# Ranking the first head pair's preparation and maxima ahead, its keys loaded by ScalarE's queue and its queries transposed first

## The chip, the cores and the metric

The kernel runs on one core of one Trainium2 chip. The metric is the device time of one execution in microseconds (us), lower is better; a set of runs is given by its median. An engine works through its own instructions strictly in the order in which the program lists them, and waits at an instruction whose inputs or buffers are not there yet.

## What is computed

Attention over pooled queries, followed by a feed-forward layer with softplus:

```python
q_pool = q.reshape(B, H, S // 2, 2, D).mean(axis=3)      # B=4, H=8, S=1152, D=64
scores = (1 / sqrt(D)) * q_pool @ k.T
scores = scores - scores.max(axis=-1)
attn = exp(scores); attn = attn / (attn.sum(axis=-1) + 1e-9)
x = (attn @ v), heads side by side                       # 2304 x 512
h = x @ w_in                                             # 512 x 2048
g = max(h, 0) + log1p(exp(-abs(h)))
out = g @ w_out                                          # 2048 x 512
```

All inputs and the output are float32 in the reference; the weights reach the kernel as 64-bit words and are decoded on the chip.

## The kernel before, in words

The work is cut into 16 units, u0 to u15, each one pair of heads of one batch, and into 8 blocks of rows of the feed-forward layer (U is the product with w_in and the softplus, D the product with w_out). For every unit there are three stages:

- **Preparation** (`prepare`, lines 540 to 649). The keys of the pair come by one DMA (L559) and the queries by six (L582 and L586) into two of the four `raw` buffers. Neighbouring queries are added (L348, the helper `tt_ways`). ScalarE takes the sum of squares of both (L437, the helper `squares`), a matmul with ones (L284) and four short VectorE instructions (L272, L292) make a power-of-two scale from them. Then keys and queries are each split into a high and a low float16 part: high by `hi_ways` (L315 on ScalarE, L319 on GpSimd, L272 on VectorE), low by `lo_ways` (L275 on VectorE). The two halves of the keys go into `kcat`, of which there is one, and a DMA transposes it into `kT` (L612); a further DMA copies its high part to `kB` (L618). The queries' high part goes into `qcat`, also one, and is transposed into `qA` (L625); their low part stays in `qlow`.
- **Maxima** (`maxima`, lines 652 to 736). The row maxima of the scores are found ahead of the attention. Per unit, 12 pairs of matmuls (L667) and 3 mixed pairs (L678) write 384 columns each into one of three PSUM banks `m`, and VectorE reduces each bank to one column (L688): 12 reduces for the first half of the rows, 15 for the second. When the 12 of the first half are there, L693 joins them, L272 and L275 (called at L696 and L698) put the result beside `qlow`, TensorE turns `qlow` (L713) and a copy (L733 on VectorE, or L730 on ScalarE) puts it into `qB`.
- **Attention** (`attention`, lines 762 to 890). For each half of the rows and each of nine key tiles: scores (L777 with `kT`, `qA`; L780 with `kB`, `qB`), the exponential on ScalarE (L787), the product with v (L795) and, in the first six units, the sums by TensorE (L802).

The order of the instructions is not written out by hand. Everything is a `task` with a rank (`prio`, the smaller goes first), the engines that could run it with a planned duration, and the tasks that it depends on. `Sched.run` plays this through once while the program is built: whenever an engine is free in that play, it takes the task of the smallest rank among those that are ready and whose buffers are free, and the instruction is then emitted. An engine is never kept free for a task that becomes ready a little later. DMAs are played as one server, `nbytes / 300 + 180` ns each, in their order of rank. So a changed rank can change the order of every later instruction, on every engine.

Ranks count key tiles of the attention: u0 starts at 0, u1 at 18, u2 at 36. A unit's preparation is ranked from the start of the unit before it (`x.was`, -18 for u0, 0 for u1, 18 for u2): loads at `was - 20`, preparation at `was - 14`, the queries' high part and their transposition one later, the maxima from `was` on. The decoding of w_in is ranked at 8, 16, ... 64 (`w_in`, lines 448 to 478, with `decode`, lines 406 to 431), that of w_out from 54 on. For u0 this gives loads at -38, preparation at -32, queries at -31, maxima at -18 to -4.8 (the mixed ones -3.6 to -2.4), the joining of the halves at -10.8 and -3.6. For u1: loads at -20, preparation at -14, queries at -13, maxima from 0 on.

Of the kernel before, what the change touches and what calls it, by code (L numbers as in the profile page):

```python
# [42 lines left out]
class Sched:  # L43
# [17 lines left out]
    def task(self, ways, deps=(), prio=0.0, take=(), give=()):  # L61
        t = Task(ways, prio, list(take), list(give))
        for d in deps:
            if d is not None:
                d.after.append(t)
                t.deps += 1
        self.tasks.append(t)
        return t
# [87 lines left out]
def pe(n, cols):  # L156
    return n * (cols / 2.4 + 2.5)
# [27 lines left out]
def tile_attention_softplus_ffn(  # L185
# [166 lines left out]
    def load(fn, nbytes, deps, prio, take):  # L352
        return task([("DMA", dma(nbytes), fn)], deps, prio, take=take)
# [186 lines left out]
    def prepare(u):  # L540
# [13 lines left out]
        x.sc = c[8]  # L554


        prio = x.was - 14.0
        r, cat = Hold(raw_r), Hold(kcat_r)
        kl = load(lambda: nc.sync.dma_start(  # L559
            out=r.item[:, 0:1152].rearrange("p (h t d) -> p h t d", h=2, t=KT),  # L560
            in_=k[b, 2 * p:2 * p + 2].rearrange("h (p t) d -> p h t d", t=KT)),
            2 * S * D * 4, [], prio - 6.0, [r])
        qr, qc = Hold(raw_r, 2), Hold(qcat_r)

        def raw():
# [52 lines left out]
                nc.sync.dma_start(out=x.kB.item[0:D, ks], in_=x.kT.item[h * D:(h + 1) * D, ks])  # L618

        x.kB_done = task([("DMA", 1500.0, high_keys)], [x.k_done], prio + 4.0, take=[x.kB])  # L620
        prio += 1.0
        y = task(hi_ways(1152, lambda: (qc.item, twice(qs()), c[5]), ("ACT", "DVE"), 1.0), [both], prio)
        x.ql_done = task(lo_ways(576, lambda: (x.qlow.item[:, :, 0:D], qs(), c[5], qc.item[:, :, 0])),
                         [y], prio, take=[x.qlow], give=[qr])
# [27 lines left out]
    def maxima(x):  # L652
        half_done, begun = [], None
        for half in range(2):
            parts = []
            first, last = ((0, 4), (4, T))[half]
            for o, t in enumerate(range(2 * half, 2 * half + 2 + half)):
                for g in range(3):
                    prio = x.was + x.early * (7.2 * half + 3.6 * o + 1.2 * g * (t < 4) + 0.6 * g * (t == 4))
                    if t < 4:  # L660
                        ps = [Hold(m_r), Hold(m_r)]

                        def mm(t=t, g=g, ps=ps):
                            for h in range(2):
                                k0 = h * KT + 3 * g
                                hs = slice(h * D, (h + 1) * D)
                                nc.tensor.matmul(  # L667
                                    out=ps[h].item[:, 0:384], lhsT=x.qA.item[hs, PLACE[h, t]],
                                    rhs=x.kT.item[hs, k0:k0 + 3].rearrange("p a b -> p (a b)"),
                                    start=True, stop=True, tile_position=(h * D, 0))  # L670
                    else:
                        ps = [Hold(m_r)]

                        def mm(t=t, g=g, ps=ps):
                            for h in range(2):
                                k0 = h * KT + 3 * g
                                hs = slice(h * D, (h + 1) * D)
                                nc.tensor.matmul(  # L678
                                    out=ps[0].item[hs, 0:384], lhsT=x.qA.item[hs, MIX, hs],
                                    rhs=x.kT.item[hs, k0:k0 + 3].rearrange("p a b -> p (a b)"),  # L680
                                    start=True, stop=True, tile_position=(h * D, h * D))

                    y = task([("PE", pe(1, 384) + 130.0, mm)], [x.q_done, x.k_done, begun], prio,
                             take=ps if begun else ps + [x.nm3], give=[x.qA, x.kT])
                    begun = begun or y
                    for h, bank in enumerate(ps):
                        c = PLACE[h, t] if t < 4 else MIX
                        parts.append(task([("DVE", dve(384), lambda c=c, g=g, bank=bank: nc.vector.tensor_reduce(  # L688
                            out=x.nm3.item[:, c, g:g + 1], in_=bank.item[:, 0:384], axis=AX.X, op=ALU.max,
                            negate=True))], [y], prio, give=[bank]))  # L690
            prio = x.was + x.early * 7.2 * (half + 1)
            ts_ = slice(first, last)
            y = small(lambda ts_=ts_: nc.vector.tensor_reduce(  # L693
                out=x.nm.item[:, ts_], in_=x.nm3.item[:, ts_], axis=AX.X, op=ALU.min), parts, prio,
# [6 lines left out]
            half_done.append(y)  # L701
        x.qB_done = [[], []]
        for half, h in ((0, None), (1, 0), (1, 1)):
            prio = x.was + x.early * 7.2 * (half + 1) + 0.2
            ps = Hold(m_r)
            n = 320 if half else 512

# [54 lines left out]
    def attention(x):  # L762
        b, p = x.b, x.p
        gate = since("u", x.u)
        for i, (t0, t1) in enumerate(HALF):
            n = (t1 - t0) * 64
            pv, acc = Hold(pv_r), Hold(acc_r)
            before = None
            sums = None
            for kt in range(KT):  # L770
                prio = x.at + x.slow * (9.0 * i + kt)
                s, pt = Hold(s_r), Hold(p_r, 2)
# [1 line left out]
                def scores(kt=kt, s=s, t0=t0, t1=t1, n=n, i=i):  # L774
                    for h in range(2):
# [4 lines left out]
                        nc.tensor.matmul(out=s.item[:, h, 0:n], lhsT=x.kB.item[0:D + 2, h * KT + kt],  # L780
                                         rhs=x.qB.item[0:D + 2, h, t0 * 64:t1 * 64], start=False, stop=True)

                y = task([("PE", pe(4, n) + 30.0, scores)], [x.kB_done, x.q2_done, *x.qB_done[i]], prio, take=[s],
                         give=[x.kT, x.kB, x.qA, x.qB])

                def exp(s=s, pt=pt, n=n):
                    nc.scalar.activation(out=pt.item[:, :, 0:n], in_=s.item[:, :, 0:n], func=ACTF.Exp,  # L787
                                         scale=x.sc)

                e = task([("ACT", act(2 * n, 1, 1), exp)], [y, x.sc_done, *gate], prio, take=[pt], give=[s])  # L790
                exps.setdefault(x.u, []).append(e)

                def product(kt=kt, pv=pv, pt=pt, n=n):
# [13 lines left out]
                def product_and_sums(kt=kt, product=product, summed=summed):  # L807

                    for part in (product, summed) if kt == 0 else (summed, product):
# [1 line left out]

                here = x.u in SUMMED
                y = task([("PE", pe(1, (6 if here else 4) * n) + (160.0 if here else 80.0), product_and_sums if here else product)],
                         [e, x.v_done], prio + 1.9,
                         take=[pv] if kt == 0 else [], give=[pt, x.v])

                if here:
# [260 lines left out]
```

## Time and profile before

| what | value |
|---|---|
| median of 3 runs | 997.37 us (988.73 to 997.45) |
| the profiled execution, its own time | 984.97 us |
| span of the profiled execution, first to last instruction | 983.3 us |
| TensorE busy | 903.1 us |
| VectorE busy | 608.3 us |
| ScalarE busy | 472.4 us |
| mean granted TensorE clock over the span | 0.979 |

All instruction times below are counted from the start of the span of the profiled execution, so they belong to 983.3 us and not to the median. The busy time of an engine is the time in which it had an instruction; TensorE is shown as busy also when it runs at the lower of its clock levels, so the duration and spacing of single matmuls has to be read beside its share.

### The profile page before, as it was taken

The page shows a single profiled execution, that of the slowest core. Times are in us where ns is not written, and L with a number is a line of the kernel's source. Part 1 is how long each engine was busy: PE and PEld are TensorE (multiplying, and loading weights), DVE is VectorE, ACT ScalarE, POOL GpSimd, SP SyncE. Part 2 cuts the span into 40 slices and gives each one's busy share as a digit, 9 for nine tenths or more (in the row PEclk, how much of TensorE's full clock was granted, in tenths as well). Part 3 has the DMA queues.
Part 4 walks back from the last instruction along what each step waited for, and adds up shares of the span by engine and source line. Part 5 has one row for each costly group of instructions (what it writes and reads, how often), then busy time and mean ns, then how long its engine had stood idle before and what let it go on. Part 6 is the DMA issues. An engine that isn't in the chain of part 4 may idle for free.

```text
span 983.3 us, 16320 instructions
## 1 busy us (share of the span) xinstructions
PE 903.1 (92%) x6426; PEld 452.8 (46%) x6426; DVE 608.3 (62%) x1301; ACT 472.4 (48%) x739; POOL 162.8 (17%) x141
## 2 busy tenths in 40 slices
PE   2799999798789999999999999999899999969998
PEld 0244344244534456444544564333654744335483
DVE  5777587877667766666664467777654657526030
ACT  4547477777765345345442354455533545322020
POOL 1000010210212411134001112344112013000000
PEclk9999999799989999999999999999999999979999
DMA  8725426456434025041310151432300300000000
GB/s 239 189 81 152 124 78 190 115 170 162 123 94 104 12 62 90 12 136 37 68 37 28 43 96 39 107 78 68 86 1 17 91 1 17 13 18 1 22 12 21
DMA packets 101581, 74.61 MB, mean 76 GB/s; under 512 B 68480, under 2 KB 82816, under 8 KB 101504
## 3 DMA queue, kind: packets, MB, share of 16 engines
q1 hardware_dynamic: 101504, 73.57, 28.3%
q8 instruction: 50, 0.82, 0.4%
q14 instruction: 27, 0.22, 0.1%
HBM read 49.81 MB, written 4.79 MB: 56 GB/s over the span
## 4 chain that ended last, share of the span: by engine, by line
PE 54%; DMA 8%; DVE 7%; ACT 4%; issue 1%; POOL 0%; SPq 0%; ACTq 0%; DVEq 0%
PE m L960 16%; PE m L1009 14%; PE pv L795 10%; DMA rinv<-scratch 5%; PE s L777 5%; PE s L780 4%; PE m L667 3%; DVE nm L688 2%; DMA scratch<-few 2%; DMA few<-rinv 1%; ACT g L1020 1%; ACT p L787 1%; DVE xT L348 1%; ACT L787 1%; DVE w L275 1%
## 5 line engine op out<-in xcount | busy, mean ns | idle before, releaser
L787 ACT ACTIVATE p<-s,cols 128x512 f32<-128x512 f32 (+1 forms) x288 | 209.5, 738 | 209.3 <-PE s L780 206.8
L688 DVE TENSOR_REDUCE nm<-m 128x1 f32<-128x384 f32 x432 | 222.6, 550 | 108.9 <-PE m L667 100.3
L795 PE MATMUL pv<-p,v 128*64 128x320 f32 (+1 forms) x1152 | 207.1, 441 | 3.4 <-ACT rinv L868 1.6
L960 PE MATMUL m<-w,gh 128*128 128x512 f16 x576 | 171.8, 380 | 0.0
L777 PE MATMUL s<-qA,kT 128*128 128x256 f16 (+1 forms) x576 | 159.4, 296 | 8.5 <-ACT p L787 8.4
L780 PE MATMUL s<-qB,kB 66*128 66x256 f16 (+1 forms) x576 | 157.8, 293 | 0.0
L348 POOL TENSOR_TENSOR acc<-acc,p 128x512 f32<-128x512 f32 (+1 forms) x73 | 104.6, 1433 | 225.2 <-ACT p L787 189.8
L1009 PEld LDWEIGHTS <-w1h 128*128 128x128 f16 x1024 | 99.7, 99 | 49.7 <-issue 25.4
L960 PE MATMUL m<-w,gl 128*128 128x512 f16 x288 | 109.1, 379 | 0.0
L1020 ACT ACTIVATE g<-m,blk 128x512 f32<-128x512 f32 (+1 forms) x80 | 51.4, 642 | 110.1 <-PE m L1009 106.3
L1009 PE MATMUL m<-xh,w1h 128*128 128x256 f16 (+1 forms) x512 | 85.4, 289 | 17.7 <-DVE xh L272 7.7
L777 PEld LDWEIGHTS <-kT 128*128 128x128 f16 x576 | 57.8, 100 | 90.4 <-issue 80.6
L667 PE MATMUL m<-kT,qA 64*128 64x384 f16 x384 | 74.3, 347 | 20.2 <-DMA qA<-qcat 9.6
L795 PEld LDWEIGHTS pv<-p,v 128*64 128x64 f32 x1152 | 58.7, 137 | 72.2 <-issue 57.6
L960 PEld LDWEIGHTS <-gh 128*128 128x128 f16 x576 | 54.1, 98 | 68.0 <-issue 11.1
L1009 PE MATMUL m<-xl,w1h 128*128 128x256 f16 (+1 forms) x512 | 85.2, 290 | 0.0
L1009 PE MATMUL m<-xh,w1l 128*128 128x256 f16 (+1 forms) x512 | 84.8, 289 | 0.0
L348 DVE TENSOR_TENSOR acc<-acc,p 128x640 f32<-128x640 f32 (+1 forms) x67 | 50.8, 758 | 45.1 <-ACT p L787 36.9
L272 DVE TENSOR_SCALAR gh<-g,blk 128x512 f16<-128x512 f32 (+1 forms) x64 | 29.4, 459 | 76.4 <-ACT g L1020 76.1
L780 PEld LDWEIGHTS <-kB 66*128 66x128 f16 x576 | 57.3, 100 | 19.3 <-issue 9.3
L275 DVE SCALAR_TENSOR_TENSOR gl<-g,blk,gh 128x512 f16<-128x512 f32 (+1 forms) x80 | 55.7, 696 | 5.1 <-ACT gh L315 2.3
L667 PEld LDWEIGHTS <-qA 64*128 64x128 f16 x384 | 19.5, 93 | 85.2 <-issue 75.3
(139 smaller groups left out, 836.3 us busy)
## 6 DMA issues: line engine op xcount, KB each, us to landing
raw<-in_k_dram SPq DMA_DIRECT2D x16, 576.0 KB
v<-in_v_dram SPq DMA_DIRECT2D x16, 576.0 KB
raw<-in_q_dram SPq DMA_DIRECT2D x64, 128.0 KB
raw<-in_moe_w_out_dram SPq DMA_DIRECT2D x16, 512.0 KB
kB<-kT SPq DMA_DIRECT2D x32, 144.0 KB
gh<-in_moe_w_in_dram SPq DMA_DIRECT2D x4, 1024.0 KB
gl<-in_moe_w_in_dram SPq DMA_DIRECT2D x4, 1024.0 KB
out_dram<-o SPq DMA_DIRECT2D x16, 256.0 KB
```

The lines of the kernel that those rows point to most:

```text
L272: nc.vector.tensor_scalar(out=out_, in0=in_, scalar1=s1, scalar2=s2, op0=op0, **kw)
L275: nc.vector.scalar_tensor_tensor(out=out_, in0=in0, scalar=s, in1=in1, op0=op0, op1=op1)
L348: e.tensor_tensor(out=o, in0=a, in1=b, op=op)
L667: nc.tensor.matmul(out=ps[h].item[:, 0:384], lhsT=x.qA.item[hs, PLACE[h, t]], rhs=x.kT.item[hs, k0:k0 + 3].rearrange("p a b -> p (a b)"), ...
L688: parts.append(task([("DVE", dve(384), lambda c=c, g=g, bank=bank: nc.vector.tensor_reduce(out=x.nm3.item[:, c, g:g + 1], in_=bank.item[:, ...
L777: nc.tensor.matmul(out=s.item[:, h, 0:n], lhsT=x.kT.item[:, h * KT + kt], rhs=x.qA.item.rearrange("p a b -> p (a b)")[:, c0:c0 + n], start ...
L780: nc.tensor.matmul(out=s.item[:, h, 0:n], lhsT=x.kB.item[0:D + 2, h * KT + kt], rhs=x.qB.item[0:D + 2, h, t0 * 64:t1 * 64], start=False, s ...
L787: nc.scalar.activation(out=pt.item[:, :, 0:n], in_=s.item[:, :, 0:n], func=ACTF.Exp, scale=x.sc)
L795: nc.tensor.matmul(out=pv.item[h * 64:(h + 1) * 64, 0:n], lhsT=x.v.item[:, h, kt], rhs=pt.item[:, h, 0:n], start=(kt == 0), stop=(kt == KT ...
L960: nc.tensor.matmul(out=ps.item[:, 0:512], lhsT=gt[:, f, t * 128:(t + 1) * 128], rhs=w2[:, f, wt, :], start=(f == 0 and m == 0), stop=(f == ...
L1009: nc.tensor.matmul(out=pv[:, f], lhsT=wt[:, kk, c0:c0 + 128], rhs=xt[:, kk, 0:w], start=(idx == 0), stop=(idx == 11))
L1020: x = task([("ACT", act(N, 1, 1), lambda: nc.scalar.activation(out=gs.item[:, 0:N], in_=ps.item[:, 0:N], func=ACTF.Softplus, scale=ih[:, g ...
```

## The change

For u0 alone, four things are altered, and one thing in the attention of all units:

- The rank of its preparation is 18 smaller: preparation at -50, loads at -56.
- Its keys are loaded by a DMA issued from ScalarE's queue and not from SyncE's, at rank -55.5, half a step behind the queries' six DMAs, which stay on SyncE's queue.
- The high part of its queries, their low part and their transposition are ranked one ahead of the keys' parts (-51) where they were one behind.
- Its maxima, the joining of the halves, the turn and the copy to `qB` are ranked 16 smaller: the matmuls and reduces at -34 to -18.4 in place of -18 to -2.4.
- In the attention each product with v now also depends on the product of the key tile before it (the name `y` is kept for it, and the scores' task is called `sc`).

```diff
-        prio = x.was - 14.0
+        prio = x.was - 14.0 - (18.0 if u == 0 else 0.0)
         r, cat = Hold(raw_r), Hold(kcat_r)
-        kl = load(lambda: nc.sync.dma_start(
+        kl = load(lambda: (nc.sync if u else nc.scalar).dma_start(
             out=r.item[:, 0:1152].rearrange("p (h t d) -> p h t d", h=2, t=KT),
             in_=k[b, 2 * p:2 * p + 2].rearrange("h (p t) d -> p h t d", t=KT)),
-            2 * S * D * 4, [], prio - 6.0, [r])
+            2 * S * D * 4, [], prio - 6.0 + (0.0 if u else 0.5), [r])
...
-        prio += 1.0
+        prio += 1.0 if u else -1.0
         y = task(hi_ways(1152, lambda: (qc.item, twice(qs()), c[5]), ("ACT", "DVE"), 1.0), [both], prio)
...
                     prio = x.was + x.early * (7.2 * half + 3.6 * o + 1.2 * g * (t < 4) + 0.6 * g * (t == 4))
+                    if x.u == 0:
+                        prio -= 16.0
...
-            prio = x.was + x.early * 7.2 * (half + 1)
+            prio = x.was + x.early * 7.2 * (half + 1) - (16.0 if x.u == 0 else 0.0)
...
-            prio = x.was + x.early * 7.2 * (half + 1) + 0.2
+            prio = x.was + x.early * 7.2 * (half + 1) + 0.2 - (16.0 if x.u == 0 else 0.0)
...
-            sums = None
+            sums = y = None
...
-                y = task([("PE", pe(4, n) + 30.0, scores)], [x.kB_done, x.q2_done, *x.qB_done[i]], prio, take=[s],
-                         give=[x.kT, x.kB, x.qA, x.qB])
+                sc = task([("PE", pe(4, n) + 30.0, scores)], [x.kB_done, x.q2_done, *x.qB_done[i]], prio, take=[s],
+                          give=[x.kT, x.kB, x.qA, x.qB])
...
-                e = task([("ACT", act(2 * n, 1, 1), exp)], [y, x.sc_done, *gate], prio, take=[pt], give=[s])
+                e = task([("ACT", act(2 * n, 1, 1), exp)], [sc, x.sc_done, *gate], prio, take=[pt], give=[s])
...
-                         [e, x.v_done], prio + 1.9,
+                         [e, x.v_done, y], prio + 1.9,
```

## Rows read from the trace of the kernel before

**Rows 1.** Part 1 of the page, and the busy time of each engine in stages of the first 74 us: stage and its length, then busy us and number of instructions of TensorE, its weight loads, VectorE, ScalarE and GpSimd, granted clock, share of the DMA engines, GB/s.

```profile
PE 903.1 (92%) x6426; PEld 452.8 (46%) x6426; DVE 608.3 (62%) x1301; ACT 472.4 (48%) x739; POOL 162.8 (17%) x141
...
0.00:19.00 19.00, 0.59 (x2) 0.50 (x2) 9.81 (x13) 8.52 (x12) 2.55 (x7) 1.00 0.81 233
19.00:36.00 17.00, 10.63 (x33) 3.20 (x34) 15.33 (x35) 7.01 (x11) 2.38 (x3) 1.00 1.02 256
36.00:47.00 11.00, 10.93 (x71) 4.46 (x69) 6.80 (x12) 7.83 (x13) 0.00 (x0) 1.00 0.47 134
47.00:56.00 9.00, 9.00 (x93) 4.38 (x86) 6.50 (x18) 4.33 (x6) 0.74 (x1) 1.00 0.39 117
```

**Rows 2.** The same for two later stages, in which w_out is decoded.

```profile
170.00:180.00 10.00, 5.54 (x44) 2.33 (x43) 8.89 (x15) 6.95 (x12) 2.19 (x2) 0.84 0.28 74
180.00:190.00 10.00, 9.92 (x64) 3.48 (x63) 8.05 (x21) 7.10 (x15) 2.03 (x2) 0.61 0.35 112
```

**Rows 3.** SyncE's DMA queue in order of time: start us, duration of the issue in us, line, transfer.

```profile
0.81 0.46 SPq L559 DMA_DIRECT2D raw<-in_k_dram  x1
1.32 0.93 SPq L582 DMA_DIRECT2D raw<-in_q_dram  x2
...
4.01 0.49 SPq L586 DMA_DIRECT2D raw<-in_q_dram  x1
...
14.15 1.88 SPq L612 DMA_TRANSPOSE kT<-kcat  x1
16.13 1.36 SPq L625 DMA_TRANSPOSE qA<-qcat  x1
18.23 1.15 SPq L618 DMA_DIRECT2D kB<-kT  x2
...
27.85 7.22 SPq L612 DMA_TRANSPOSE kT<-kcat  x1
37.29 1.14 SPq L618 DMA_DIRECT2D kB<-kT  x2
```

**Rows 4.** ScalarE in order of time: start us, duration us, line, operation, in brackets the idle time before it and what ended it.

```profile
0.80 1.28 ACT L437 ACT_TABLE_LOAD   x1 [0.80 <-PEq L1063]
4.99 1.16 ACT L437 ACTIVATE kcat<-raw 128x1152 f16<-128x1152 f32 x1 [2.91 <-DMA raw<-in_k_dram]
6.06 0.19 ACT L437 ACTIVATION_READ_ACCUMULATOR kcat<-raw 128x1 f32 x1
8.26 0.68 ACT L437 ACTIVATE qcat<-raw 128x576 f16<-128x576 f32 x1 [2.01 <-DVE raw L348]
8.84 0.19 ACT L437 ACTIVATION_READ_ACCUMULATOR qcat<-raw 128x1 f32 x1
```

**Rows 5.** VectorE and TensorE up to the first matmul of the maxima, in order of time, columns as in rows 4.

```profile
7.46 0.76 DVE L348 TENSOR_TENSOR raw<-raw 128x576 f32<-128x576 f32 x1 [1.50 <-DMA raw<-in_q_dram]
...
11.38 2.69 DVE L275 SCALAR_TENSOR_TENSOR kcat<-raw,cols,kcat 128x576 f16<-128x576 f32 x2
...
13.99 0.81 DVE L275 SCALAR_TENSOR_TENSOR qlow<-raw,cols,qcat 128x576 f16<-128x576 f32 x1
...
19.28 0.50 PE L667 MATMUL m<-kT,qA 64*128 64x384 f16 x2 [9.61 <-DMA qA<-qcat]
```

**Rows 6.** VectorE in order of time from the first reduce to the copy that the first scores wait for; in the piece left out between 21.19 and 24.76 stand reduces and four further short instructions of u1's scale (0.16, 0.16, 0.16 and 0.21 us).

```profile
19.81 1.02 DVE L688 TENSOR_REDUCE nm<-m 128x1 f32<-128x384 f32 x2 [0.38 <-PE m L667]
21.12 0.16 DVE L272 TENSOR_SCALAR cols<-m 128x2 f32<-128x2 f32 x1 [0.28 <-PE m L284]
...
23.71 0.21 DVE L272 TENSOR_SCALAR cols<-cols 128x1 f32<-128x1 f32 x1
...
24.76 0.81 DVE L275 SCALAR_TENSOR_TENSOR kcat<-raw,cols,kcat 128x576 f16<-128x576 f32 x1
...
26.42 1.40 DVE L275 SCALAR_TENSOR_TENSOR kcat<-raw,cols,kcat 128x576 f16<-128x576 f32 x1
...
28.67 0.80 DVE L275 SCALAR_TENSOR_TENSOR qlow<-raw,cols,qcat 128x576 f16<-128x576 f32 x1
...
31.17 0.70 DVE L272 TENSOR_SCALAR raw<-raw 128x1024 int32<-128x1024 int32 x1 [0.76 <-ACT raw L413]
31.79 0.15 DVE L693 TENSOR_REDUCE nm<-nm 128x4 f32<-128x12 f32 x1
31.87 1.00 DVE L688 TENSOR_REDUCE nm<-m 128x1 f32<-128x384 f32 x2
...
32.86 1.21 DVE L275 SCALAR_TENSOR_TENSOR raw<-gh,raw 128x1024 int32<-128x1024 int32 x1
...
34.07 1.01 DVE L688 TENSOR_REDUCE nm<-m 128x1 f32<-128x384 f32 x2
35.00 0.67 DVE L733 CAST qB<-m 66x512 f16<-66x512 f32 x1
```

**Rows 7.** TensorE in order of time: the first scores of u0, and scores and products further on.

```profile
35.54 0.39 PE L777 MATMUL s<-qA,kT 128*128 128x256 f16 x1
...
43.01 0.42 PE L777 MATMUL s<-qA,kT 128*128 128x256 f16 x1
43.22 0.42 PE L780 MATMUL s<-qB,kB 66*128 66x256 f16 x1
...
45.25 1.12 PE L795 MATMUL pv<-p,v 128*64 128x256 f32 x4
...
48.27 0.28 PE L780 MATMUL s<-qB,kB 66*128 66x256 f16 x1
48.39 0.27 PE L777 MATMUL s<-qA,kT 128*128 128x256 f16 x1
...
49.33 0.65 PE L795 MATMUL pv<-p,v 128*64 128x256 f32 x4
...
95.07 0.81 PE L795 MATMUL pv<-p,v 128*64 128x320 f32 x4 [1.60 <-ACT rinv L868]
```

**Rows 8.** The start of the decoding of w_in on ScalarE, VectorE's first reduce of u1's maxima, and TensorE's first scores of u1, in order of time.

```profile
30.02 1.12 ACT L413 ACTIVATE raw<-gh 128x1024 f32<-128x1024 f32 x1 [5.12 <-DVE nm L688]
...
49.07 0.56 DVE L688 TENSOR_REDUCE nm<-m 128x1 f32<-128x384 f32 x1 [1.00 <-PE m L667]
...
74.25 0.28 PE L777 MATMUL s<-qA,kT 128*128 128x256 f16 x1
```

## The prediction

> **What bounds the kernel now.** I read the busy times first. TensorE is busy 92% of the span, VectorE 62%, ScalarE 48% [rows 1]. So the kernel is short of TensorE time, and what can be won is the time in which TensorE has nothing to do. The stages show where one lump of that lies: in the first 19 us TensorE works 0.59 us, between 19 and 36 us 10.63 of 17, and from 36 us on it is nearly full [rows 1]. The head is what the change aims at.
>
> Next I followed the head in order of time, engine by engine. The first matmul of the maxima starts at 19.28 us; what ended TensorE's wait is the landing of the transposed queries [rows 5], whose transposition was issued at 16.13, behind that of the keys at 14.15 [rows 3]. The first scores start at 35.54 [rows 7], directly behind the copy into `qB` at 35.00 [rows 6]. Between the two, VectorE is the limit: it is busy 15.33 us of the 17 from 19 to 36 [rows 1]. Not all of that is u0's maxima. There stand the scale and the low parts of u1 and the decoding of w_in [rows 6]. TensorE's speed changes too: matmuls of 256 columns start 0.21 us apart at 43 us (1.2 columns per ns, the level of 1.2 GHz) and 0.12 us apart at 48.3 (the level of 2.4 GHz) [rows 7]. The stage table gives a granted clock of 1.00 in both [rows 1]; the spacing decides.
>
> **The change part by part.** *Loads.* Before, the keys land first: ScalarE squares them from 4.99 to 6.25. The queries land at 7.46 [rows 5], are added for 0.76, and are squared from 8.26 to 9.03 [rows 4]; the scale needs both. After, the queries are issued 0.5 us earlier (1.32 becomes 0.81, and the last of the six starts at 3.5, not 4.01 [rows 3]). The keys' issue on ScalarE, about 0.5 us as on SyncE, is covered: ScalarE idles 2.91 us before 4.99 with its table load (1.28) already done [rows 4]. But ScalarE's order turns round. In the planner's play the queries load first (2.15 us, plus 0.96 lag), are added (0.75) and are ready to be squared at about 3.9; the keys, second on the one DMA server, at 5.25. So the keys' squares (1.25 us with the read of the sum) now come behind the queries'. If the queries land as long after their last issue as before (3.45 us), at 6.95, their squares end at 8.52 and the keys' at 9.78: 0.75 later than 9.03. If they land at 5.5, with nothing ahead of them in the queue, the keys' squares end at 8.3: 0.7 earlier. I take +0.2, nearer to the first, because both transfers now share the engines.
>
> The Trainium skill (DMA: Bandwidth & Descriptors, Issuing engines are not separate DMA queues) speaks against this part: DMAs issued from several engines run on the same 16 engines and interleave, and only the issue time is saved. No row here has two issuing engines; by that rule this term would be the +0.75.
>
> *Queries first.* `hi_ways` lets the queries' high part take ScalarE at once; the keys' second half goes to GpSimd or VectorE, at no cost on the path. But the queries' low part (0.81) now also ranks ahead of the keys' second low part, where it stood behind the two (2.69, from 11.38) at 13.99 [rows 5]. The keys' transposition is therefore issued 0.8 later: 14.15 + 0.2 + 0.8 = 15.15. It landed 4.05 us after its issue (14.15; the copy to `kB` that waits for it went out at 18.23 [rows 3]), so now at 19.2. The queries, transposed from about 12.5 on, are then long there. Maxima started at 19.28 and start at about 19.2 to 19.3: the keys take the queries' place as what is late, and the step is worth 0. Bounds: -0.8 if the low parts keep their order, +1.0 if the overlap with GpSimd slows them as it did one of u1's (1.40 against 0.81 [rows 6]) and a bit more.
>
> *Maxima ranked ahead.* This is the main term. VectorE's time from 19.81 to 35.67 that is not u0's first half: five short instructions of u1's scale, 0.85 (0.16 four times, 0.21); three low parts of u1, 0.81 + 1.40 + 0.80 = 3.01; the decoding's shift with the wait before it, 0.70 + 0.76, and its 1.21 [rows 6]. Together 6.53. All of it now ranks behind every reduce of u0. It doesn't all vanish, since the planner never keeps an engine free. It plans 550 ns for a reduce, and 292 for a pair's matmuls, doubled to 585 while it holds TensorE to be cold. From the end of a pair's first reduce the next pair is ready after 50 + 585 + 55 = 690 ns, while the second reduce takes 550: some 140 ns of gap, and what is ready and lower in rank slips in. I count the scale's five and one low part as slipping in (0.85 + 0.81 = 1.66), and the decoding not: it needs a `raw` buffer, which u1's low parts free, and began at 30.02 [rows 8], right behind the last of them at 29.47. That leaves 6.53 - 1.66 = 4.87. The reduces of the second half between the joining and the copy (1.00 and 1.01 [rows 6]) stay: each step of the joining leaves a planned gap of 40 ns. Bounds: -6.5 if nothing slips in, -2.5 if all three low parts do and one decoding step follows.
>
> *The product's new dependency.* Products of a half come out of one TensorE queue in order of rank, which rises with the key tile; the planner's lag from TensorE to TensorE is 0. So it costs nothing, and as a guard it removes nothing.
>
> *What is late next.* u1's preparation moves behind u0's 27 reduces: 19.3 + 27 x 0.51 + 0.85 = 33.9, and 3.0 more for its low parts, 37, where it was 29.5. Before, its keys took 9.44 us from issue to landing (27.85 to 37.29 [rows 3]), beside the w_in loads. Landing at 37 + 9.4 = 46.4 in the worst case; its first reduce was at 49.07 [rows 8], and would be wanted at 44.2. Its first scores come 25 us after that (74.25 [rows 8]), for 27 reduces of 0.51, 14 us. So 2 us of lateness is covered. VectorE idles 4.2 us from 36 to 47 and 2.5 to 56 [rows 1], which takes the work moved.
>
> **Sum:** the loads' +0.2 is inside the 19.2 already, so the start of the maxima gives 0 and the stretch behind it -4.9 (4.87): 983.3 becomes 978.4 us. From 36 us TensorE is full, so a start 4.9 us earlier goes through. The profiled execution took 984.97, the median is 997.37, 12.4 above it. Taking the difference to the median: 992.5 us. The bounds add up to -0.7 - 0.8 - 6.5 = -8.0 and +0.75 + 1.0 - 2.5 = -0.75, so 989.4 to 996.6.
>
> **The rivals.** *Given back* (about 997). TensorE starts earlier but at the low level. Four products take 1.12 us there and 0.65 above [rows 7], so work at the low level goes at 0.58 of the speed; if the level still rises at 46.7, the earlier 4.9 us are worth 2.0 less, and if the planner's gaps also take two low parts and a decoding step more (2.5), nothing is left. For it: gaps are there. Against it: the level rose behind a stretch in which TensorE was nearly full (10.93 of 11 us [rows 1]), and it will be full earlier. The Trainium skill (TensorE: Matmul & The Clock Gate, What's actually happening) has activity release the throttle; by that the rise moves with the work, and the trace's rise behind a full stretch agrees.
>
> *A better order further on* (about 984). All later instructions are put in order anew. From 170 to 180 us TensorE leaves 4.46 us of ten unused, and from 180 to 190 its granted clock is 0.61, 3.9 us lost of ten [rows 2]; a wait of 1.60 us at 93.5 is followed by a stretch at the low level [rows 7]. If the new order avoids one such stop, 8.4 comes on top: -13.3. If it only moves it, nothing does. The profile can't tell which.
>
> *Slower* (about 1007). The place is w_in's decoding. It starts when u1's low parts free `raw`, at 30.02 [rows 8]; now at 37 + 0.6 + 0.5, some 38, 8.1 later, while attention is 4.9 earlier. If the decoding is what the first feed-forward block waits for, the end moves by +8.1, and about 2 for the low level after such a stop. It decides only if the decoding has less than 13 us of slack there. Against it: its eight pieces are ranked eight key tiles apart, so they are spread by rank, and VectorE has idle time right behind.
>
> **How the numbers follow.** Forecast 0.5, given back 0.2, better order 0.2, slower 0.1. About 1% is what a measurement here can tell from no change, since three runs spread over 0.9%. Beyond -10 us lie the better order and a small tail of the forecast, for runs at the profiled execution's level: 0.24. Beyond +10 lies most of the slower case: 0.09. The rest is 0.67. The range takes in the better order and the profiled level (984.97 - 4.9 = 980) below, and given back with a spread of 3 above: 980 to 1000. The forecast's own range is 989.4 to 996.6.
>
> **What the profile would show.** Loads: the keys' squares on ScalarE behind the queries', the scale's matmul near 9.3 us. Queries first: their transposition issued by 12.5, the keys' at about 15, the first maxima within 0.8 us of 19.3. Maxima: u1's low parts and the decoding behind u0's reduces, first scores near 30.6 and not 35.5. Given back would show first scores early but u1's first scores still at 74; slower, a wait of TensorE behind the decoding. I am wrong if the first scores move and the end does not, or if the stages after 150 us change by more than the head.

## The result, and the profile after

| | before | after |
|---|---|---|
| median of 12 runs each, us | 991.44 (987.52 to 997.45) | 1002.04 (997.27 to 1008.71) |
| ratio, 95% interval | 1 | 1.0108 (1.0081 to 1.0136) |
| span of the profiled execution, us | 983.3 | 1007.0 |
| mean granted TensorE clock over the span | 0.979 | 0.959 |

The changed kernel is 1.1% slower, 10.6 us by the medians. The forecast was 992.5, with 980 to 1000 as range: the time lies above it. The profiled execution of after took 1008.71 us, the longest of its twelve, and that of before, 984.97, was shorter than all of its twelve, so the two traces stand 23.7 us apart, about twice what the medians do; they show the places of the loss better than its size.

Part 1 of the page of after answers to the first line of [rows 1]: TensorE is busy longer (921.5 for 903.1) with the same 6426 matmuls, while VectorE and ScalarE have slightly less to do.

```profile
PE 921.5 (92%) x6426; PEld 458.7 (46%) x6426; DVE 603.7 (60%) x1300; ACT 465.0 (46%) x729; POOL 164.2 (16%) x150
```

Matmuls that last longer point to the clock. The stages of after (columns as in [rows 1]) show where:

```profile
0.00:19.00 19.00, 0.59 (x2) 0.60 (x3) 9.97 (x14) 6.38 (x10) 2.81 (x8) 1.00 0.72 203
19.00:36.00 17.00, 9.38 (x29) 2.82 (x29) 14.56 (x34) 7.56 (x11) 0.98 (x2) 1.00 1.01 274
36.00:47.00 11.00, 11.00 (x72) 5.11 (x71) 7.96 (x20) 7.16 (x12) 0.00 (x0) 1.00 0.70 210
...
140.00:150.00 10.00, 6.43 (x60) 2.22 (x57) 4.24 (x12) 3.09 (x5) 0.53 (x1) 1.00 0.87 124
150.00:160.00 10.00, 9.30 (x28) 3.02 (x28) 9.66 (x29) 4.29 (x6) 0.24 (x1) 0.53 0.77 232
160.00:170.00 10.00, 10.00 (x61) 3.47 (x59) 5.08 (x8) 3.69 (x7) 3.49 (x4) 0.50 0.25 70
...
210.00:220.00 10.00, 9.18 (x65) 3.87 (x64) 7.86 (x21) 7.94 (x17) 0.40 (x2) 0.60 0.66 199
220.00:230.00 10.00, 10.00 (x65) 3.56 (x62) 4.86 (x12) 4.30 (x8) 1.85 (x3) 0.55 0.43 121
```

The head is not better: from 19 to 36 us TensorE works 9.38 us where it worked 10.63 [rows 1]. It isn't much worse either. The loss is far behind it. From 140 to 150 us TensorE lacks 3.57 us of work, and from 150 to 170 it is busy but at the lower of its levels (0.53, 0.50); the same level returns from 210 to 230. Before had 1.00, 1.00 and 0.87 in the stages from 140 to 170, and 1.00 in both from 210 to 230:

```profile
150.00:160.00 10.00, 9.74 (x97) 4.67 (x95) 9.08 (x21) 9.99 (x19) 0.55 (x2) 1.00 0.83 225
160.00:170.00 10.00, 8.69 (x80) 3.92 (x76) 5.67 (x22) 6.57 (x12) 0.00 (x0) 0.87 0.54 176
...
210.00:220.00 10.00, 9.63 (x95) 4.21 (x92) 6.49 (x13) 7.42 (x15) 0.49 (x1) 1.00 0.39 131
220.00:230.00 10.00, 8.99 (x86) 3.84 (x86) 9.10 (x25) 6.67 (x13) 1.42 (x1) 1.00 0.35 117
```

Before has a dip of this kind, a lack of work and then the lower level, from 170 to 190 us (0.84 and 0.61 [rows 2]), where after has 0.95 and 1.00, so the whole span has to be compared. An estimate from the mean granted clocks: (1 - 0.959) x 1007 = 41 us of work at full level are lost to the clock, against (1 - 0.979) x 983 = 21 before. The difference is 20 of the 23.7 us.

The head of after in order of time, all engines (columns as in [rows 4]; from line 660 on its lines are two further down than before's), answers to [rows 3] to [rows 7]:

```profile
6.69 1.28 ACT L437 ACT_TABLE_LOAD   x1 [6.69 <-DMA raw<-in_q_dram]
...
7.99 0.68 ACT L437 ACTIVATE qcat<-raw 128x576 f16<-128x576 f32 x1
8.67 1.15 ACT L437 ACTIVATE kcat<-raw 128x1152 f16<-128x1152 f32 x1
...
9.96 0.59 PE L284 MATMUL m<-cols,ones 128*128 128x2 f32 x2 [9.96 <-ACT kcat L437]
...
15.66 1.75 SPq L612 DMA_TRANSPOSE kT<-kcat  x1
...
19.59 0.50 PE L669 MATMUL m<-kT,qA 64*128 64x384 f16 x2 [9.05 <-DMA kT<-kcat]
...
24.43 0.76 DVE L348 TENSOR_TENSOR raw<-raw 128x576 f32<-128x576 f32 x1 [1.23 <-DMA raw<-in_q_dram]
...
27.08 0.81 DVE L275 SCALAR_TENSOR_TENSOR kcat<-raw,cols,kcat 128x576 f16<-128x576 f32 x1
...
28.74 0.81 DVE L275 SCALAR_TENSOR_TENSOR kcat<-raw,cols,kcat 128x576 f16<-128x576 f32 x1
...
30.40 0.81 DVE L275 SCALAR_TENSOR_TENSOR qlow<-raw,cols,qcat 128x576 f16<-128x576 f32 x1
...
32.08 0.69 DVE L272 TENSOR_SCALAR raw<-raw 128x1024 int32<-128x1024 int32 x1
...
33.76 1.22 DVE L275 SCALAR_TENSOR_TENSOR raw<-gh,raw 128x1024 int32<-128x1024 int32 x1
...
36.44 0.40 PE L779 MATMUL s<-qA,kT 128*128 128x256 f16 x1
```

The keys' squares stand behind the queries', as forecast; the table load, which was done at 2.1 [rows 4], now stands behind the wait for the queries. The first matmul of the maxima waits for the keys and no longer for the queries. But between the reduces there are again all three low parts of u1, the decoding of w_in and, new, the addition of u2's queries with a wait for their DMA. The first scores come at 36.44, not at 30.6; before it was 35.54 [rows 7].

VectorE and TensorE of after around the first loss, from 148 to 173 us, each in order of time:

```profile
148.84 0.42 DVE L348 TENSOR_TENSOR xT<-xT,rinv 128x256 f32<-128x256 f32 x1 [4.98 <-DMA rinv<-scratch]
...
151.33 5.19 DVE L690 TENSOR_REDUCE nm<-m 128x1 f32<-128x384 f32 x11
...
149.85 0.32 PE L669 MATMUL m<-kT,qA 64*128 64x384 f16 x1 [3.47 <-DVE bm L272]
...
151.15 6.44 PE L669 MATMUL m<-kT,qA 64*128 64x384 f16 x14
...
159.06 0.40 PE L779 MATMUL s<-qA,kT 128*128 128x256 f16 x1
...
162.28 1.12 PE L797 MATMUL pv<-p,v 128*64 128x256 f32 x4
...
172.50 0.65 PE L797 MATMUL pv<-p,v 128*64 128x256 f32 x4
```

VectorE stands 4.98 us at a multiplication by the reciprocal sums, whose DMA has not landed. Behind it in VectorE's queue stand u3's maxima. TensorE runs out of u2's scores, gets one matmul of the maxima, then the maxima alone, fourteen in 6.44 us, at the pace of the reduces. u3's first scores start at 159.1 (before at 149.7), and the products take 1.12 us, the lower level, until some point between 162 and 172.5.

### The profile page after: what moved, and what is told of

It reads as the page before. It is cut to its first block, busy times and chain, and to the rows that moved or that the text cites. A ratio compares the mean times of both kernels' runs of the same rounds, so it can differ in the third digit from the quotient of the medians.

```text
span 1007.0 us, 16333 instructions
## 1 busy us (share of the span) xinstructions
PE 921.5 (92%) x6426; PEld 458.7 (46%) x6426; DVE 603.7 (60%) x1300; ACT 465.0 (46%) x729; POOL 164.2 (16%) x150
## 4 chain that ended last, share of the span: by engine, by line
PE 57%; DMA 13%; DVE 7%; ACT 5%; issue 3%; POOL 1%; SPq 1%; ACTq 0%; DVEq 0%; POOLq 0%
PE m L962 15%; PE m L1011 15%; PE pv L797 11%; DMA rinv<-scratch 8%; PE s L779 5%; PE s L782 4%; PE m L669 3%; DVE nm L690 3%; DMA scratch<-few 2%; PE pv L804 2%; DMA few<-rinv 1%; ACT g L1022 1%; ACT p L789 1%; DMA kT<-kcat 1%; DMA raw<-in_moe_w_out_dram 1%
## 5 line engine op out<-in xcount | busy, mean ns | idle before, releaser
L797 PE MATMUL pv<-p,v 128*64 128x320 f32 (+1 forms) x1152 | 209.7, 446 | 3.7 <-ACT rinv L870 2.0
L779 PE MATMUL s<-qA,kT 128*128 128x256 f16 (+1 forms) x576 | 161.8, 299 | 4.7 <-ACT p L789 4.6
L782 PE MATMUL s<-qB,kB 66*128 66x256 f16 (+1 forms) x576 | 160.3, 297 | 0.2 <-ACT qB L732 0.2
L348 POOL TENSOR_TENSOR acc<-acc,p 128x512 f32<-128x512 f32 (+1 forms) x69 | 98.3, 1424 | 229.2 <-ACT p L789 194.1
L669 PE MATMUL m<-kT,qA 64*128 64x384 f16 x384 | 79.8, 356 | 24.5 <-DVE nm L690 11.1
L1011 PE MATMUL m<-xh,w1l 128*128 128x256 f16 (+1 forms) x512 | 87.0, 294 | 0.0
L348 DVE TENSOR_TENSOR acc<-acc,p 128x512 f32<-128x512 f32 (+1 forms) x71 | 53.6, 755 | 44.1 <-ACT p L789 38.3
L275 DVE SCALAR_TENSOR_TENSOR gl<-g,blk,gh 128x512 f16<-128x512 f32 (+1 forms) x80 | 55.7, 696 | 9.3 <-POOL gh L319 3.3
L1011 PEld LDWEIGHTS <-w1l 128*128 128x128 f16 x512 | 51.6, 101 | 14.7 <-issue 1.2
```

Source lines behind the costliest of these rows:

```text
L275: nc.vector.scalar_tensor_tensor(out=out_, in0=in0, scalar=s, in1=in1, op0=op0, op1=op1)
L348: e.tensor_tensor(out=o, in0=a, in1=b, op=op)
L669: nc.tensor.matmul(out=ps[h].item[:, 0:384], lhsT=x.qA.item[hs, PLACE[h, t]], rhs=x.kT.item[hs, k0:k0 + 3].rearrange("p a b -> p (a b)"), ...
L779: nc.tensor.matmul(out=s.item[:, h, 0:n], lhsT=x.kT.item[:, h * KT + kt], rhs=x.qA.item.rearrange("p a b -> p (a b)")[:, c0:c0 + n], start ...
L797: nc.tensor.matmul(out=pv.item[h * 64:(h + 1) * 64, 0:n], lhsT=x.v.item[:, h, kt], rhs=pt.item[:, h, 0:n], start=(kt == 0), stop=(kt == KT ...
L1011: nc.tensor.matmul(out=pv[:, f], lhsT=wt[:, kk, c0:c0 + 128], rhs=xt[:, kk, 0:w], start=(idx == 0), stop=(idx == 11))
```

## The experiments

Two theories stood against each other. **Theory 1:** the order of all later instructions, which the planner derives anew from the changed ranks, makes the loss; the changed head itself costs about nothing. **Theory 2:** the head itself (the loads, u1's work pushed aside, w_in's pieces in the `raw` buffers) makes it. To tell them apart, the planner was played through without emitting, with the ranks of before and with those of after; every task thus has a planned engine, start and end in both plans. The instructions were then emitted in a chosen order of these starts. With one whole plan this gives exactly that kernel's order, and the products' new dependency moves no instruction in it. Ratios are to the kernel before, with 95% intervals; above 1 is slower.

**Head against rest.** The first kernel takes u0's preparation, maxima and turn from the plan of after, with the keys on ScalarE's queue, and all else from before's; the second is the reverse; the third moves only the keys' DMA.

```diff
-        sd.run()
+        before, after = sd.play(False), sd.play(True)
+        key = {n: (after if n in head else before)[n] for n in before}   # the reverse in the second
+        sd.follow(key)
```

> The planner is played twice, with the ranks of before and of after. u0's preparation, maxima and turn (and the keys' DMA on ScalarE's queue) stand as in the order of after, every other instruction as in the order of before; the printed order differs from that of before in 85 lines, all in the head. Theory 1 (the order behind the head makes the loss): first scores at 36 to 37 us as in after, time within 0.3% of before. Theory 2 (the head itself makes it): 0.8 to 1.4% slower than before, as after is.

> The reverse: u0's preparation, maxima and turn in the order of before, with the keys' DMA on SyncE's queue, every other instruction in the order of after. Theory 1: 0.8 to 1.4% slower than before, though its first scores come at 35 to 36 us. Theory 2: within 0.3% of before.

> The order of before, instruction by instruction; only u0's keys are loaded by a DMA from ScalarE's queue. Theory 1: first scores up to 1.3 us later or 0.5 earlier (the table load may move behind a wait, 1.28 us), time within 0.2% of before. Theory 2: this part makes the loss, 0.5 to 1.1% slower.

Measured: 992.38 us, 1.0018 (0.9984 to 1.0051), for the head of after in before's order; 1008.92, 1.0188 (1.0140 to 1.0235), for the head of before in after's order; 991.77, 1.0016 (0.9985 to 1.0047), for the queue alone. The loss goes with the order of the rest. Theory 2 falls. The two parts don't simply add, though: the second kernel is slower than its expected range and 0.8 points slower than after itself (1.0108), with intervals that do not overlap, so behind after's rest the head of before is the worse one.

ScalarE with the queue alone, in order of time (the planner's replay stands in the file, so the lines of these kernels are numbered otherwise):

```profile
1.30 1.28 ACT L505 ACT_TABLE_LOAD   x1 [1.30 <-PEq L1144]
...
4.96 1.16 ACT L505 ACTIVATE kcat<-raw 128x1152 f16<-128x1152 f32 x1 [2.38 <-DMA raw<-in_k_dram]
...
7.39 0.68 ACT L505 ACTIVATE qcat<-raw 128x576 f16<-128x576 f32 x1 [1.18 <-DVE raw L416]
```

The keys' squares stay where they were (4.96 for 4.99), the queries' come 0.87 us earlier (8.26 [rows 4]); 0.51 of that is the issue of the keys that SyncE no longer makes ahead of them. The Trainium skill (DMA: Bandwidth & Descriptors, Issuing engines are not separate DMA queues) says that only the time of issue is saved; these rows agree in kind, with 0.36 us more than that.

**Other orders from the same ranks.** If the order is the cause, a change that means nothing should move the time as well. One planned duration of one task was raised by 0.3 us, in before (twice) and in after (twice); the planner then derives the rest anew.

```diff
+        t = sd.tasks[1626]            # u1's copy of its first product; 1560: a DMA; 1661: a later task
+        t.ways = [(e, d + 300.0, f) for e, d, f in t.ways]
         sd.run()
```

> Before, with one planned duration altered: the copy of u1's first product is priced 0.3 us dearer in the planner's play. The instructions do the same work, and the order is the same up to some 80 us; behind it 1172 lines of the printed order differ. Theory 1 (a newly derived order alone moves the time by about 1%, without any reason in the head): outside 0.997 to 1.003 of before, either way. Rival (the planner's orders are all about equally good, and that of after is bad by what the changed head does to it): within 0.3% of before.

> Before, with the planned duration of one DMA (the spreading of u0's first reciprocal sums) 0.3 us longer in the planner's play; 1524 lines of the printed order differ, all behind 75 us. Theory 1 (a newly derived order alone moves the time by up to about 1% either way): anywhere from 0.988 to 1.018 of before, outside 0.997 to 1.003 more likely than not. Rival (orders are about equally good): within 0.3%.

> After, with the planned duration of one copy (of u1's first product) 0.3 us longer in the planner's play; the head is that of after, 1228 lines behind it differ. Theory 1: the time is that of a new order, 0.99 to 1.015 of before, and better than after at even chance or more. Theory 2 (what the changed head does lasts): 1.008 to 1.014, as after.

> After, with the planned duration of another copy (of u1's second product) 0.3 us longer in the planner's play; the head is that of after, 1182 lines behind it, later than in the run before, differ. Theory 1: 0.99 to 1.015 of before. If the crowding of w_in in front of u3's maxima is the larger part of the loss, it stays here, since the order changes only behind some 105 us: 1.003 to 1.014. Theory 2: 1.008 to 1.014.

Measured: before with one duration changed 980.33 us, 0.9915 (0.9883 to 0.9947); with another 992.79, 1.0024 (0.9987 to 1.0060); after with the first 1007.68, 1.0181 (1.0139 to 1.0223); with the third 989.26, 0.9998 (0.9971 to 1.0024). Durations that mean nothing moved before by -0.85 and +0.24 points (the second within its interval), and after by +0.73 and -1.10: about as far as the change did. The time goes with the clock here: by the estimate used above, the profiled executions, one of each, lose 18, 26, 31 and 41 us to it, from the quickest kernel of the four to the slowest.

The last of the four is the sharpest: its instructions are those of after up to about 105 us, and it has before's time. So what the change does in the first 105 us, the head with u1's and w_in's work in it, does not bind the kernel to the loss. What that part costs by itself a single order can't tell; in before's order the head alone cost 0.2%, with an interval up to 0.5% (1.0018 above). Nor is it shown that after's ranks are as good as before's on average: the three orders derived from after's ranks lie at 1.0108, 1.0181 and 0.9998, the three from before's at 1, 0.9915 and 1.0024, too few to tell. The window of the last from 150 to 160 us, to be read beside the one of after above:

```profile
150.00:160.00 10.00, 8.85 (x53) 3.73 (x52) 7.89 (x22) 6.90 (x13) 1.12 (x1) 0.66 0.78 226
```

53 matmuls for 28; from 160 to 170 its clock is 1.00 again, where after has 0.50.

**What in the order.** Four kernels alter after's order at the place of the loss. The first gives the two multiplications that wait 2.92 and 4.98 us (at 132.69 and 148.84) to GpSimd; the second also puts u3's first maxima 14 us earlier; the third ranks u3's loads ten key tiles later, so that w_in's pieces get the `raw` buffers first, and plans anew. The expectations split theory 1: 1a, the two waits make the loss; 1b, it is spread over many places; 1c, w_in's pieces crowd VectorE in front of u3's maxima.

```diff
+        plan[n] = (a, "POOL", z + 400.0)                  # first and second: two tasks
+        plan[t.n] = (m, e, m + z - a)                     # second: u3's maxima, m = a - 14 us
-            2 * S * D * 4, [], prio - 6.0, [r])
+            2 * S * D * 4, [], prio - 6.0 + (10.0 if u == 3 else 0.0), [r])    # third
```

> The order of after, with two instructions moved from VectorE to GpSimd: the multiplications by the reciprocal sums in u1's second and u2's first half, before which VectorE idled 2.92 and 4.98 us for a DMA (at 132.69 and 148.84 us). Theory 1a (these two waits hold up u3's maxima and make the low clock after them): u3's first scores at 148 to 153 us in place of 159, and 0.6 to 1.2% faster than after, so within 0.5% of before. Theory 1b (the loss is spread over many places): not more than 0.3% faster than after, 0.8 to 1.4% slower than before.

> The order of after with the two multiplications on GpSimd as before, and u3's matmuls and reduces of the first half 14 us earlier in the order of TensorE and VectorE, ahead of the w_in pieces that crowd there. Theory 1c: u3's first scores at 144 to 150 us with no run of bare maxima before them, 0.3 to 0.8% faster than with the two multiplications alone, so 0.998 to 1.004 of before. Theory 1b: no faster than with the two alone (1.005 to 1.010).

> After with one rank altered: u3's keys and queries are loaded at rank 26, not 16, so that w_in's pieces (16, 24, 32) come to the four raw buffers before them. Theory 1c (in after u3's early load, 32 us and not 58, keeps the raw buffers from w_in; its second piece is decoded at 85 us and not 44, four pieces crowd VectorE between 100 and 143 us in front of u3's maxima, TensorE runs dry at 146 and then stays at the low clock): second piece decoded before 65 us, u3's first scores at 140 to 150 us, time 0.8 to 2% faster than after, at or below before (0.985 to 1.003 of before). Theory 1b (spread over many places): 1.004 to 1.014 of before.

Measured: 998.75 us, 1.0071 (1.0041 to 1.0101); 999.20, 1.0103 (1.0058 to 1.0149); 991.26, 1.0006 (0.9974 to 1.0039). Without the two waits 0.4 points come back, with intervals that overlap. VectorE's other waits for that DMA grew meanwhile (59.0 us in total are left of 61.1), and in the first kernel u3's first scores come at 156.3 and not by 153, with the clock from 150 to 160 us still at 0.58. The earlier maxima bring nothing more. The third recovers all, and its window from 150 to 160 us is full:

```profile
150.00:160.00 10.00, 10.00 (x104) 4.21 (x102) 8.45 (x17) 8.47 (x15) 0.24 (x1) 1.00 0.76 193
```

Its own dip lies earlier, from 130 to 140 us (6.43 us of work in ten, clock 0.66). But behind the shifted loads the planner derives the whole order anew, so this kernel doesn't isolate w_in. VectorE spends 9.5 us on w_in from 100 to 147 us before, 19.0 after, 5.7 here; but 19.1 in the last of the four kernels with a changed duration, which is as quick as before. That crowding alone does not set the time.

The fourth moves all of VectorE's multiplications by reciprocal sums 5 us later in its order (28 instructions), in after's plan, in before's, and in the plan of before with the one duration changed.

```diff
+        key[t.n] = (a + 5000.0, e, z + 5000.0)            # each of these multiplications
```

> The order of after; only VectorE's multiplications by the reciprocal sums stand 5 us later in its order (64 lines of the printed order, 28 instructions moved). In after VectorE idles 61.1 us in front of them for the DMA that brings the sums, in before 44.6: the planner takes that DMA to be there after 1.56 us. Theory 1d (these waits, and the low clock that they lead to, are what makes the order of after worse): their idle time falls below 25 us and the time to 0.995 to 1.004 of before. Theory 1b (the order of after is worse in many places, these waits carry only the 0.4% that two of them carried): 1.004 to 1.012.

> The same shift in the order of before (68 lines). Theory 1d: the idle time of 44.6 us falls below 20, and the time by 0.5 to 1.5% (0.985 to 0.995 of before), less than in after, where there is more of it. Theory 1b: within 0.4% of before.

> The order that was 0.85% faster than before (one planned duration altered), with the same shift of the multiplications. Theory 1d: another 0.5 to 1.5%, 0.977 to 0.987 of before. Theory 1b: within 0.4% of 0.9915.

Measured: 982.33 us, 0.9920 (0.9894 to 0.9946), in after's order; 973.24, 0.9824 (0.9782 to 0.9866), in before's; 964.57, 0.9733 (0.9693 to 0.9772), in the third, which beats both kernels. All three are quicker than either theory expected. VectorE's waits for that DMA before, after, in after shifted and in before shifted (engine and line waited for: us in total, times, longest us):

```profile
DVE xT L348 <- DMA rinv<-scratch: 44.6, 24, 7.9
```

```profile
DVE xT L348 <- DMA rinv<-scratch: 61.1, 24, 7.7
```

```profile
DVE xT L416 <- DMA rinv<-scratch: 7.9, 1, 7.9
```

```profile
DVE xT L416 <- DMA rinv<-scratch: 8.3, 1, 8.3
```

All but one of the 24 waits are gone, and each order gains 1.8 to 1.9 points. So the waits are a loss that both kernels have, not the difference between them: 0.992 to 0.9824 are still 0.96 points apart. That these waits make the slowdown, the theory on which this experiment was built, falls too. In the shifted after the first dip is shorter but still there (clock 0.50 from 150 to 160 us, 0.98 from 160 to 170), and the second is seen beside the shifted before, in the stages from 200 to 220 us:

```profile
200.00:210.00 10.00, 8.26 (x59) 3.10 (x57) 7.63 (x17) 9.27 (x18) 1.52 (x2) 0.73 0.70 151
210.00:220.00 10.00, 10.00 (x61) 4.18 (x62) 4.75 (x12) 5.08 (x10) 1.85 (x2) 0.50 0.47 154
```

```profile
200.00:210.00 10.00, 10.00 (x110) 4.52 (x112) 6.50 (x18) 8.19 (x15) 1.48 (x1) 1.00 0.58 211
210.00:220.00 10.00, 9.63 (x90) 4.00 (x91) 7.80 (x17) 6.67 (x14) 1.80 (x2) 1.00 0.46 129
```

120 matmuls for 200 in the same 20 us: a short lack of work, and then the lower level while TensorE is shown as full.

**What an early start is worth.** In before's order, u0's first-half maxima, joining, turn and copy were put ahead of everything on their engines; the second kernel also puts that half's scores, exponentials and products 9 us earlier.

```diff
+        first = {t.n for t in sd.tasks if t.what in (('max', 0, 0), ('turn', 0, 0))}
+        move = lambda n: 1e6 if n in first else 9000.0 if n in near else 0.0    # near: second kernel only
+        key = {n: (a - move(n), e, z - move(n)) for n, (a, e, z) in key.items()}
```

> The order of before, with the twelve matmul pairs, reduces, joining, turn and copy of u0's first half put ahead of everything else on TensorE, VectorE and ScalarE that isn't needed for them; the planner's filling of gaps is switched off there. It does what the prediction took the change to do. The prediction's step that a start so many us earlier goes through to the end: first scores at 27 to 31 us in place of 35.5, time 0.4 to 0.9% faster than before (0.991 to 0.996). Rival (the gain of the head is given back later, as TensorE waits there for others): first scores at 27 to 31, time within 0.3% of before.

> As with the forced head, and u0's scores, exponentials and products of the first half stand 9 us earlier in the planned order too, ahead of the second half's maxima on TensorE. The prediction's step that a start some us earlier goes through to the end: first scores at 28 to 31 us, u0's second half from 46 to 50 us in place of 55.7, 0.4 to 0.7% faster than before. Rival (given back: the second half waits for its maxima, which stand behind u1's preparation and w_in on VectorE): first scores at 28 to 31, second half not before 54, time within 0.4% of before.

Measured: 995.94 us, 1.0046 (1.0008 to 1.0083), and 995.57, 1.0076 (1.0044 to 1.0108), each beside its own runs of before. VectorE and then TensorE of the first of the two:

```profile
20.16 5.67 DVE L762 TENSOR_REDUCE nm<-m 128x1 f32<-128x384 f32 x12 [4.95 <-PE m L741]
...
35.92 0.94 PE L741 MATMUL m<-kT,qA 64*128 64x384 f16 x2 [5.55 <-DVE nm L762]
...
38.39 0.40 PE L853 MATMUL s<-qA,kT 128*128 128x256 f16 x1
```

The twelve reduces run without a break and `qB` is there before 28 us, yet the scores start at 38.39: in TensorE's queue they stand behind a pair of second-half matmuls, which wait 5.55 us for VectorE. TensorE of the second:

```profile
28.58 0.40 PE L854 MATMUL s<-qA,kT 128*128 128x256 f16 x1
...
35.06 1.12 PE L872 MATMUL pv<-p,v 128*64 128x256 f32 x4 [4.59 <-ACT p L864]
...
57.07 0.43 PE L854 MATMUL s<-qA,kT 128*128 128x320 f16 x1
```

Here the scores do start 7 us earlier; but the first products wait 4.59 us for the exponential. On ScalarE that exponential stands behind u1's high parts, which wait 9.50 us for u1's scale, and behind the first decoding of w_in; it starts at 34.34. The second half starts at 57.07 (before at 55.7), with TensorE at the lower level (0.50 from 57 to 62 us; before has 1.00 from 55 to 66), and the kernel is 0.8% slower. Both times are slower than either side expected, and the first kernel's scores did not come at 27 to 31 us. In these two orders an earlier start, of up to 7 us for the scores, was worth nothing.

## Why the prediction was wrong, point by point

- **The base.** The sum was made against the profiled execution and carried to a median of 997.37, of three runs. Over 12 runs that median is 991.44. The forecast of 992.5 thus meant a gain of 4.9; measured is a loss of 10.6, so the miss is 15.5 and not the 9.5 that 992.5 and 1002.04 show.
- **Loads, +0.2 and its bounds: the right mechanism, the size slightly off.** The order on ScalarE turned as the planner's play said (queries' squares 7.99, keys' 8.67), and the scale's matmul came at 9.96, not near 9.3 (9.08 before: +0.88, just past the bound of +0.75). "With its table load already done" named a cover, and the cover failed: the load stands behind the first wait of the turned order, and its 1.28 us end at 7.97. In the kernel that moved the queue alone the table load is back at 1.30 and nothing is lost. This term is not where the time went.
- **Queries first, 0: right.** The keys took the queries' place as what is late. Their transposition went out at 15.66 (forecast 15.15), the maxima started at 19.59 (19.2 to 19.3).
- **Maxima, -4.87: the first step that failed.** "All of it now ranks behind every reduce of u0", with 1.66 us counted as slipping back. All of it slipped back: three low parts 2.43, the decoding 0.69 and 1.22, the scale's five 0.89, and with them u2's query addition, 0.76 after 1.23 of waiting, sum to 7.2 us, against 6.53 before. The gap of some 140 ns was worked out rightly, and so was the rule that an engine is never kept free. What was missed: whatever slips in is longer than the gap, so it delays the next reduce and with it the next pair, and so opens the next gap. Maxima to scores took 16.85 us (16.26 before). In these runs a rank did not keep such a chain together; only the forced order did, 5.67 us for twelve reduces.
- **"A start 4.9 us earlier goes through": failed as well.** The forced starts show it: with the scores at 28.58 TensorE waits for the exponential, and the time rises. The "given back" rival had this outcome, a start that is worth nothing. One of its two reasons, that the gaps take more, is what came in after; the other, a level that still rises at 46.7, is not: it rose at about 44.7 in after and by 43.9 in the second forced kernel. What it did not have are the waits behind the start, in the queues, and the new stretch at the lower level behind them.
- **The order further on: the step that cost the range.** The prediction saw that every later instruction is ordered anew, and named the dip at 170 to 190 us [rows 2], but priced it in one direction: "if it only moves it, nothing does". An order that makes a new dip was not priced. The runs show one: 41 us lost to the clock in after and 21 before, by the estimate above. The prediction's own last sign of being wrong, stages after 150 us that change by more than the head, is what came. The four orders with one planned duration changed scatter by up to about 1% around the orders that they were made from. That after is one draw from such a scatter, on the slow side, fits all runs but is argued and not shown; a hit or a miss by 1% would then be luck.
- **The slower rival (1007)** gave a time close to the profiled one, but by another mechanism: w_in's decoding began at 30.92 (30.02 before [rows 8]), not at 38.
- **What stays open.** Which of the swapped instructions behind 105 us start the dips at 146 and near 204 us. Removing the two waits gives 0.4 points, later loads of u3 give all, and with all but one of VectorE's waits for the sums gone both dips are still there, the first one shorter. A longer planned time for that DMA, with the order derived from it, was not tried.

## What to carry to other kernels

Where a greedy planner orders every later instruction, a rank is no local edit: replay the old order with only the intended part moved. Alter one planned duration by a little, several times, to see how far the time scatters, before a per cent is put down to the idea. A chain that is to run as one stretch needs the order itself, since ranks alone let longer work into each small gap. What slips in can be read before any run: the play that fixes the order needs no chip. And look for what the planner has wrong: here the landing of one DMA, and with VectorE's waits for it moved away 1.8 to 1.9 points came off each of the three orders in which that was tried.

## What was not expected of the hardware

The DMA `rinv<-scratch` (SyncE's queue; L885 in after) is planned at 1.56 us from issue to use (0.96 and 0.6). It was issued at 124.04 and 142.94, and the multiplications that wait for it started at 132.69 and 148.84: 8.6 and 5.9 us.

TensorE stayed at the lower level from about 151 to 171 us although its busy share was 9.30 and 10.00 of 10, with matmuls of the maxima 0.46 us apart and then scores 0.21 apart. In the head of after the level rose at about 44.7 us (scores 0.21 apart become 0.11), 8.3 us behind the first scores; before it was between 47.3 and 48.2, some 12 behind them. The Trainium skill (TensorE: Matmul & The Clock Gate, What's actually happening) has activity release the throttle; by these rows the share shown as busy does not tell when.
